# Query weights fused from DMA-transposed raw blocks, and the first two tiles of each layer without the residual sum on TensorE

## The chip, the cores and the metric

The kernel runs on one NeuronCore of a Trainium2 chip. The core has a matrix engine (TensorE, PE in the profile; its weight loads are the row PEld), a vector engine (VectorE, DVE), an activation engine (ScalarE, ACT), a general engine (GpSimd, POOL) and a queue engine (SyncE, SP) from which all DMA of this kernel is issued. The engines run their instruction streams in order and meet at semaphores. The metric is the device time of one execution in microseconds, as the median of several runs.

## What is computed

Two layers, each a linear attention (A) with softmax feature maps and a bilinear gated block (B). Both layers use the same weights. There are 2048 rows (16 tiles of 128), a width of 576, 32 heads of 18, and a hidden width of 4608.

```python
def A(x, wqkv, w_phi, wo):
    q, k, v = split_heads(x @ wqkv)                       # each (32 heads, 2048, 18)
    pq = einsum("bhsd,hdf->bhsf", q, w_phi)               # the kernel folds w_phi into wq and wk
    pk = einsum("bhsd,hdf->bhsf", k, w_phi)
    phi_q = concat([softmax(pq), softmax(-pq)])
    phi_k = concat([softmax(pk), softmax(-pk)])
    kv = einsum("bhsf,bhsd->bhfd", phi_k, v)
    z  = einsum("bhsf->bhf", phi_k)
    o = einsum("bhqf,bhfd->bhqd", phi_q, kv) / (einsum("bhqf,bhf->bhq", phi_q, z)[..., None] + 1e-6)
    return merge_heads(o) @ wo

def B(x, w_gate, w_up, w_down):
    return ((x @ w_gate) * (x @ w_up)) @ w_down

for _ in range(2):
    x = x + A(layernorm(x), ...)
    x = x + B(layernorm(x), ...)
```

Since q = LN(x) wq and pq = q w_phi per head, pq = LN(x) Wq with Wq = wq times a block-diagonal matrix of w_phi. That product, made once at the start for the q and for the k columns of wqkv, is called the fusion below.

## The kernel before

A Python scheduler records all instructions. Each piece of the work is a generator ("thread") that yields operations with rough durations, waits for events and takes buffers from pools; the scheduler places whichever can begin first by its own estimate. What it places is fixed in the program: on the chip each engine runs its list in that order. So a change of one thread also changes where the others stand.

The stages: all 16 tiles pass the k side of layer 1 (normalise, project to k and v, two softmaxes, add to kv); then a barrier masks kv into the block-diagonal BD; then for each pair of tiles the q side gives the attention output, and a block of gate and up projections (a "row") follows, then the down product. While a row runs, projections of other tiles are put between its matmuls. The k side of layer 2 runs inside the rows of layer 1.

The fusion for q and k, one 128-row block (kt) of the raw weights at a time. The rows of BDphi are in five groups of seven heads (126 columns):

```python
def t_fuse(self, which):
    ...
    if which == "q":
        yield ("wait", ("ain", 1, s.fq))                  # fq = 1: after tile 1 of the k side
    yield ("go", s.t_fuse2(which), ...)
    for kt in range(5):
        wt = yield ("acq", "wt")                          # two buffers
        (_, bank), = yield ("acqn", ["pb"], 1)
        # PE: 5 transposes of Wraw[:, kt, 126 columns] into one bank
        # ACT: 2 copies, bank -> WT[:, wt]
        yield ("rel", "pb", bank)

def t_fuse2(self, which):
    for kt in range(5):
        for half in range(2):
            (_, bank), = yield ("acqn", ["pb"], 1)
            # PE: groups 0..2 or 3..4: bank[:, c:c+n] = WT[:, wt, t, :]^T @ BDphi[:, t, 0:n]
            # ACT or DVE: copy of 378 or 198 columns, bank -> Wq[:, kt]
```

The load thread brings raw q weights with five loads after the sixth pair of x tiles; all transfers stand in one SP queue:

```python
for b in range(3, NB):
    yield ("wait", ("xT", 1, b - 3))
    yield from xload(b)
    if b == 5:
        for kt in range(5):
            yield from rawload("q", kt)
    if b == 6:
        yield from w5(s.Wo, s.A_wo, "Wo", "wo")
```

A query projection of a later tile, made ahead and stored, takes one of NPQ = 2 tokens and two of the eight PSUM banks:

```python
def t_qproj(self, L, st_):
    ...
    tok = yield ("acq", "pq")
    gots = yield ("acqn", ["pb"], 2, True)
    yield from s.proj(st_, s.Wq, "Wq", banks)             # 10 matmuls of 288 columns
    # ACT: 2 copies, bank -> xT[st_] (reused as store)
    yield ("rel", "pq", tok)
```

Tiles 0 and 1 of a layer lie on the way to the first row. Their attention output is transposed on TensorE, and before the change their residual sum is made there:

```python
def t_aout(self, L, st_):
    ...                                                   # numerator and denominator in 2 banks
    alts = [("dve", den)]                                 # +1e-6, reciprocal
    if st_ < 2: alts.append(("act", lnd))                 # or Ln and Exp on ScalarE
    # DVE: 2 products o = num * (1/den)
    if st_ < 2:
        # PE: 6 transposes of o, ACT: copy to oT
        for h in range(2):
            # PE: bank[h] = ident^T @ x_sb[st_, half h]   (start=True, stop=False)
        for h in range(2):
            yield from s.proj(..., s.Wo, ..., h, False)   # added to the same bank
        yield ("sig", ("xp", L, st_))
        for h in (1, 0):
            # ACT: copy bank[h] -> x_sb
        yield ("wait", ("bn", ...)); release both banks
        return
    # other tiles: proj, then DVE: x_sb = bank + x_sb
```

The normalisation of these two tiles (t_ln with fast=True) takes its statistics from the PSUM banks as soon as "xp" is signalled:

```python
src = s.ps[:, banks[h], 0:288] if banks else x_sb[...]
Op(bn_stats(st, src))                                     # DVE, 2 of them
...                                                       # aggregate, Ln, Exp, x -> xln (576 columns)
# PE: 6 transposes of xln, ACT: copy to xT
```

Of the kernel before, what the change touches and what calls it, by code (L numbers as in the profile page):

```python
# [491 lines left out]
NP = NF // 2  # L492
# [56 lines left out]
class K:  # L549
    def __init__(self, nc, A_x, A_wqkv, A_w_phi, A_wo, B_w_gate, B_w_up, B_w_down, out):  # L550
# [16 lines left out]
        self.NPQ = 2  # L567
# [3 lines left out]
        self.fq = 1  # L571
# [13 lines left out]
    def alloc(self):  # L585
# [5 lines left out]
        self.eps6 = A("eps6", [128, 1], F32)  # L591
        self.mask9 = A("mask9", [128, NK, GH], BF16)
        self.BD = A("BD", [128, NK, GH, CW], BF16)
        self.kvacc = A("kvacc", [128, NK, KW], F32)
        self.x_sb = A("x_sb", [128, NS, D], BF16)
# [16 lines left out]
        self.mask = AT("mask", [TW, TW], BF16, a0 + 1280 + 512 + 192)  # L612
        self.wdr = A("wdr", [128, self.NWD, CH, D], BF16)
# [43 lines left out]
        sc.pool("pq", self.NPQ)  # L657
# [7 lines left out]
        self.xbank = {}  # L665
# [6 lines left out]
        self.g_out = g("out")  # L672
        self.g_et = [g("et%d" % i) for i in range(self.NET)]
        self.g_ot = [g("ot%d" % i) for i in range(self.NOT)]
        self.raw_keys = [("mask",), ("BDphi",), ("onesf",), ("wst",), ("WT", 0), ("WT", 1)] + [("Wraw", 0, w_, k_) for w_ in ("q", "k") for k_ in range(5)]
# [12 lines left out]
    def t_init(self):  # L688
# [3 lines left out]
            Op(100, lambda e: e.memset(s.eps6[:], 1e-6), writes=[("eps6",)]),  # L692
            Op(200, lambda e: e.memset(s.Wk[:, 4, :], 0.0), writes=[("Wk", 0)]),
        ])
# [49 lines left out]
    def t_load(self):  # L744
# [24 lines left out]
        yield from grp("wphi", items, ("ld", "wphi"))  # L769
        for kt in range(5):  # L770
            yield from rawload("k", kt)
# [10 lines left out]
        for b in range(3, NB):  # L782
            yield ("wait", ("xT", 1, b - 3))
            yield from xload(b)
            if b == 5:
                for kt in range(5):
                    yield from rawload("q", kt)
            if b == 6:
                yield from w5(s.Wo, s.A_wo, "Wo", "wo")
# [14 lines left out]
    def t_fuse(self, which):  # L804
# [4 lines left out]
        if which == "q":  # L809
            yield ("wait", ("ain", 1, s.fq))  # L810
        yield ("go", s.t_fuse2(which), s.fqp if which == "q" else 8, "fuse2" + which)
        for kt in range(5):
# [16 lines left out]
            yield ("sig", ("wt", which, kt))  # L829

# [33 lines left out]
    blocks5 = [(k, 0, 128, 128 * k + 128) for k in range(4)] + [(4, 0, 64, 576), (4, 64, 128, 576)]  # L864

    def t_ln(self, tiles, sig, fast=False, slot=None, banks=None):
# [14 lines left out]
        for j in js:  # L883
            for h in range(2):
                if banks is None:
                    src, rd, ex = x_sb[:, ss[j], 288 * h:288 * h + 288], [("x", ss[j], 0), ("x", ss[j], 1)], []
                else:
                    src, rd, ex = s.ps[:, banks[h], 0:288], [("pbd", banks[h])], [("pb", banks[h])]
                ops.append(Op(d_dve(288), (lambda e, j=j, h=h, src=src: e.bn_stats(st[:, sl[j], 6 * h:6 * h + 6], src)),  # L889
                              reads=rd, writes=[("st", sl[j], h)], excl=ex))  # L890
        yield ("ops", "dve", ops)
        if banks is not None:
            yield ("sig", ("bn",) + sig[0])
# [15 lines left out]
        for j in js:  # L909
# [8 lines left out]
                                                                 ALU.add, ALU.mult)) for a, b, c in ((0, 576, 0), (576, 640, 512))[:2 - fast]]  # L918
            yield ("alt", [(eng, [Op(d, em[i], reads=[("x", ss[j], 0), ("x", ss[j], 1), ("nmean", sl[j]), ("rstd", sl[j])], writes=[("xln", sl[j])]) for i, d in enumerate(dur)])
                           for eng, dur in (("pool", (800, 200)[:2 - fast]), ("dve", (400,)))[:1 + fast]] + ([("act", act)] if boot else []))  # L920
        for j in js:
            if fast:
                (_, bank), = yield ("acqn", ["pb"], 1)
                P = s.psb16[bank]
                yield ("ops", "pe", [Op(60, (lambda e, j=j, k=k, P=P, r0=r0, r1=r1, c1=c1: e.transpose(P[r0:r1, 128 * k:128 * k + 128], xln[:, sl[j], 128 * k:c1], s.ident[:])),
                                        reads=[("xln", sl[j]), ("ident",)], writes=[("pbd", bank)], excl=[("pb", bank)]) for k, r0, r1, c1 in s.blocks5])
# [13 lines left out]
    def proj(self, st_, Wm, km, banks, src=None, keys=None, only=None, fresh=True):  # L940
# [4 lines left out]
        full = [Op(d_pe(N), (lambda e, k=k, h=h: e.matmul(s.ps[:, banks[h], 0:N], L[:, k, :], Wm[:, k, N * h:N * h + N], start=(k == 0 and fresh), stop=(k == 4))),  # L945
# [78 lines left out]
    def t_qproj(self, L, st_):  # L1024
# [6 lines left out]
        tok = yield ("acq", "pq")  # L1031
# [8 lines left out]
        yield ("rel", "pq", tok)  # L1040
# [110 lines left out]
    def t_kv(self, b):  # L1151
# [4 lines left out]
        for bi in range(3):  # L1156
# [10 lines left out]
            else:  # L1167
                em = (lambda e, pv=pv, kv=kv: e.tensor_tensor(kv, pv, kv, ALU.add))
            yield ("ops", "dve", [Op(d_dve(3 * KW), em, reads=[("kv", bank)] + ([("kvacc", bi)] if b else []),
                                     writes=[("kvacc", bi)], excl=[("pb", bank)])])  # L1170
# [6 lines left out]
    def t_barrier(self, L):  # L1177
# [3 lines left out]
        for bi in range(3):  # L1181
# [9 lines left out]
            yield ("alt", [(eng, [Op(dur, em, reads=rd + [("mask9",)], writes=[("BD", bi)], excl=ex)])  # L1191
# [6 lines left out]
    def t_aout(self, L, st_):  # L1198
# [40 lines left out]
        for i, (k, j, h, n) in enumerate(todo):  # L1239
# [10 lines left out]
        nv = [s.ps[:, bank, 0:16 * CW].rearrange("p (h c) -> p h c", c=CW) for bank in banks]  # L1250
        denk = [("den", ob, 0), ("den", ob, 1)]
        den = [Op(d_dve(16) + 80, (lambda e, i=i: e.tensor_scalar(s.den[:, ob, 16 * i:16 * i + 16], nv[i][:, :, DH:CW].rearrange("p h c -> p (h c)"), 1e-6, None, ALU.add)),
                  reads=[("pbd", banks[i])], writes=[("den", ob, i)], excl=[("pb", banks[i])]) for i in range(2)]
        den.append(Op(6.3 * 32 + 10, (lambda e: e.reciprocal(s.den[:, ob, :], s.den[:, ob, :])), reads=denk, writes=denk))
        alts = [("dve", den)]
        if st_ < 2:
            lnd = [Op(210, (lambda e, i=i: e.activation(s.den[:, ob, 16 * i:16 * i + 16], nv[i][:, :, DH:CW].rearrange("p h c -> p (h c)"), ACTF.Ln, bias=s.eps6[:, 0:1])),
                      reads=[("pbd", banks[i]), ("eps6",)], writes=[("den", ob, i)], excl=[("pb", banks[i])]) for i in range(2)]
            lnd.append(Op(230, (lambda e: e.activation(s.den[:, ob, :], s.den[:, ob, :], ACTF.Exp, scale=-1.0)), reads=denk, writes=denk))
            alts.append(("act", lnd))  # L1260
        yield ("alt", alts)
# [6 lines left out]
        if st_ >= 2:  # L1268
            ops.append(Op(130, (lambda e: e.tensor_copy(o[:, 576:640], o[:, 512:576])), reads=okeys, writes=okeys))
# [5 lines left out]
        if st_ < 2:  # L1275
            (_, bank), = yield ("acqn", ["pb"], 1)
            P = s.psb16[bank]
            yield ("ops", "pe", [Op(60, (lambda e, k=k, P=P, r0=r0, r1=r1, c1=c1: e.transpose(P[r0:r1, 128 * k:128 * k + 128], o[:, 128 * k:c1], s.ident[:])),
                                    reads=okeys + [("ident",)], writes=[("pbd", bank)], excl=[("pb", bank)]) for k, r0, r1, c1 in s.blocks5])
# [15 lines left out]
        if st_ < 2:  # L1295
            s.xbank[(L, st_)] = banks
            for h in range(2):
                bank = banks[h]
                yield ("ops", "pe", [Op(d_pe(288), (lambda e, h=h, bank=bank: e.matmul(s.ps[:, bank, 0:288], s.ident[:], s.x_sb[:, st_, 288 * h:288 * h + 288], start=True, stop=False)),
                                        reads=[("ident",), ("x", st_, 0), ("x", st_, 1)], writes=[("pbd", bank)], excl=[("pb", bank)])])  # L1300
            for h in range(2):
                yield from s.proj(st_, s.Wo, "Wo", banks, s.oT[:, oTb, :, :], [("oT", oTb)], h, False)
# [9 lines left out]
            for bank in banks:  # L1312
                yield ("rel", "pb", bank)
# [379 lines left out]
```

## Time and profile before

| | us |
|---|---|
| median of 3 runs | 1116.06 (1114.43 to 1116.64) |
| span of the profiled execution | 1114.3 |
| PE / DVE / ACT / POOL busy in it | 1072.3 / 592.0 / 376.5 / 311.5 |
| first gate matmul of layer 1 | 119.11 |
| last down matmul of layer 1 to first gate matmul of layer 2 | about 620.4 to 654.74 |

How to read the profile: times are microseconds from the start of the span. The page gives busy time of each engine, then the span in 40 slices of 27.9 us with one digit each (9 is 90% or more). In a line of the timeline stand the start, the busy time, the engine, the line of the kernel (L856), the operation, output and inputs, their shapes, the count, and in brackets the idle time of the engine just before and what ended it. In a table by stretch a line holds the stretch and its length, then busy time and instruction count for PE, PEld, DVE, ACT and POOL, the clock granted to TensorE, the DMA share and GB/s. In the chain of waits a line holds a start, a duration, an engine and a group. Names: ss are softmax sums, mxmn maxima and minima, dd the exponentials, psb the projections in SBUF, st the layernorm statistics, xln the normalised rows, xT and oT transposed rows.

### The profile page before, as it was taken

The numbers are of one execution on the slowest core, as the hardware profiler recorded it, in microseconds if no ns is written. First come the engines' busy times: TensorE is split into PE (matmuls) and PEld (weight loads), VectorE is DVE, ScalarE is ACT, GpSimd is POOL, SyncE is SP. The second block draws the span as 40 slices with busy tenths as digits, with TensorE's granted clock in tenths as the row PEclk, the third lists the DMA queues.
The fourth block names the chain that finished last, engine by engine and source line by source line (L and its number), as shares of the span: only waits on it lengthen the run. The fifth ranks groups of instructions, "written<-read, shape, count | busy, mean of one in ns | idle before, by whom it ended". The sixth has DMA issues, their size and how long they took to land.

```text
span 1114.3 us, 33775 instructions
## 1 busy us (share of the span) xinstructions
PE 1072.3 (96%) x15300; PEld 837.1 (75%) x15362; DVE 592.0 (53%) x1190; ACT 376.5 (34%) x867; POOL 311.5 (28%) x332
## 2 busy tenths in 40 slices
PE   5798999999999999999999899999999999999998
PEld 4566886868687786868787678696969696969685
DVE  7798744647466564646443575444535353524231
ACT  7786631414233241414332463131313130402120
POOL 5595512414242332413321252121212030300000
PEclk9699999999999999999999999999999999999999
DMA  8952127273452637262532313817272726262504
GB/s 191 265 210 65 28 43 204 47 202 49 138 107 73 156 37 199 47 191 39 138 89 78 115 24 47 214 36 215 36 209 41 192 58 192 58 177 52 181 24 139
DMA packets 181034, 128.23 MB, mean 115 GB/s; under 512 B 99354, under 2 KB 179738, under 8 KB 179738
## 3 DMA queue, kind: packets, MB, share of 16 engines
q1 hardware_dynamic: 180890, 126.07, 44.3%
q8 instruction: 120, 1.97, 0.7%
q14 instruction: 24, 0.20, 0.1%
HBM read 100.73 MB, written 2.36 MB: 93 GB/s over the span
## 4 chain that ended last, share of the span: by engine, by line
PE 82%; DVE 9%; ACT 4%; DMA 2%; issue 1%; POOL 1%; SPq 0%; DVEq 0%; ACTq 0%
PE ps L1383 46%; PE ps L1453 20%; PE ps L957 6%; PE ps L1456 4%; PE ps L945 3%; DVE ss L1072 2%; PE ps L1244 1%; DVE dd L1004 1%; PE ps L1125 1%; ACT hT L1429 1%; DMA oT<-dd 1%; DVE hT L1431 1%; DMA wdr<-in_B_w_down_dram 1%; DVE mxmn L990 1%; DVE mxmn L985 1%
## 5 line engine op out<-in xcount | busy, mean ns | idle before, releaser
L1383 PE MATMUL ps<-xT,Wu 64*128 64x256 bf16 x4608 | 581.9, 269 | 0.0
L1383 PE MATMUL ps<-xT,Wg 64*128 64x256 bf16 x4608 | 580.2, 269 | 0.8 <-ACT xT L927 0.8
L1383 PEld LDWEIGHTS ps<-xT,Wu 64*128 64x128 bf16 x4608 | 431.7, 94 | 22.6 <-DVE hT L1431 1.6
L1383 PEld LDWEIGHTS ps<-xT,Wg 64*128 64x128 bf16 x4608 | 427.5, 94 | 27.0 <-issue 3.3
L1429 ACT CAST hT<-ps 128x512 bf16<-128x512 f32 x288 | 167.9, 583 | 567.3 <-PE ps L1383 532.6
L1431 DVE TENSOR_TENSOR hT<-ps,hT 128x512 bf16<-128x512 f32 x288 | 196.9, 689 | 216.8 <-ACT hT L1429 216.0
L1453 PE MATMUL ps<-wdr,hT 128*128 128x512 bf16 x913 | 237.2, 380 | 0.4 <-DMA wdr<-in_B_w_down_dram 0.4
L1383 PE MATMUL ps<-xT,Wr 64*128 64x256 bf16 x1152 | 188.2, 269 | 0.0
L1456 PE MATMUL ps<-wdr,hT 128*128 128x64 bf16 x960 | 185.0, 193 | 2.8 <-issue 0.3
L1453 PEld LDWEIGHTS ps<-wdr,hT 128*128 128x128 bf16 x960 | 93.8, 98 | 109.6 <-DMA wdr<-in_B_w_down_dram 1.0
L1083 POOL TENSOR_TENSOR dd<-dd,ss 128x576 bf16<-128x576 bf16 x118 | 136.4, 1179 | 130.0 <-ACT ss L1079 123.0
L1054 POOL TENSOR_TENSOR dd<-xT,mxq 128x576 bf16<-128x576 bf16 x56 | 63.9, 1163 | 321.6 <-DVE mxq L1050 321.6
L1478 DVE TENSOR_TENSOR x_sb<-ps,x_sb 128x512 bf16<-128x512 f32 x32 | 22.0, 686 | 224.0 <-PE ps L1456 224.0
L917 POOL TENSOR_SCALAR xln<-x_sb,nmean,rstd 128x576 bf16<-128x576 bf16 x104 | 62.6, 607 | 172.4 <-ACT rstd L906 108.4
L1072 DVE TENSOR_REDUCE ss<-dd 128x64 f32<-128x1152 bf16 x61 | 82.2, 1348 | 26.3 <-ACT dd L1066 26.0
L1456 PEld LDWEIGHTS ps<-wdr,hT 128*128 128x128 bf16 x960 | 94.3, 98 | 0.0
L1383 PEld LDWEIGHTS ps<-xT,Wr 64*128 64x128 bf16 x1152 | 81.3, 94 | 5.2
L1064 ACT ACTIVATE dd<-dd 128x576 bf16<-128x576 bf16 x61 | 41.7, 684 | 48.9 <-DVE dd L1004 31.8
L1453 PE MATMUL ps<-wdx,hT 128*128 128x512 bf16 x177 | 50.8, 380 | 0.0
L995 POOL TENSOR_TENSOR dd<-psb,mxmn 128x576 bf16<-128x576 bf16 x24 | 27.9, 1164 | 77.0 <-DVE mxmn L985 77.0
L889 DVE BATCH_NORM_STATS2 st<-x_sb 128x6 f32<-128x288 bf16 x120 | 46.0, 445 | 3.7 <-DMA x_sb<-in_A_x_dram 3.6
L957 PE MATMUL ps<-Wo,oT 64*128 64x288 bf16 x504 | 43.5, 283 | 1.4 <-DMA oT<-dd 0.5
(118 smaller groups left out, 979.3 us busy)
## 6 DMA issues: line engine op xcount, KB each, us to landing
wdr<-in_B_w_down_dram SPq DMA_DIRECT2D x240, 288.0 KB, 3.5
wdx<-in_B_w_down_dram SPq DMA_DIRECT2D x48, 288.0 KB, 3.5
Wg<-in_B_w_gate_dram SPq DMA_DIRECT2D x4, 1152.0 KB, 15.3
Wu<-in_B_w_up_dram SPq DMA_DIRECT2D x4, 1152.0 KB, 17.6
x_sb<-in_A_x_dram SPq DMA_DIRECT2D x8, 288.0 KB, 3.2
out_dram<-x_sb SPq DMA_DIRECT2D x16, 144.0 KB, 2.3
Wraw<-in_A_wqkv_dram SPq DMA_DIRECT2D x8, 144.0 KB, 3.2
xT<-xln SPq DMA_TRANSPOSE x58, 2.7
```

What stands on the lines that cost most here:

```text
L889: ops.append(Op(d_dve(288), (lambda e, j=j, h=h, src=src: e.bn_stats(st[:, sl[j], 6 * h:6 * h + 6], src)), reads=rd, writes=[("st", sl[j], ...
L917: em = [(lambda e, j=j, a=a, b=b, c=c: e.tensor_scalar(xln[:, sl[j], a:b], x_sb[:, ss[j], c:c + b - a], s.nmean[:, sl[j]:sl[j] + 1], rstd[ ...
L957: out.append(Op(61, (lambda e, h=h, k=k, st=(i == 0 and k == 0), sp=(i == 1 and k == 3): e.matmul(s.ps[:, banks[h], 0:N], L[r, k, :], Wm[r ...
L1054: yield ("ops", "pool", [Op(1150, (lambda e, d=d, mb=mb: e.tensor_tensor(d, p3, mb, ALU.subtract)), reads=[("xT", st_), ("mq", mq, br)], w ...
L1064: yield ("ops", "act", [Op(590, (lambda e: e.activation(de2, de2, ACTF.Exp, scale=-1.0)), reads=s.ddk(sm, 1), writes=s.ddk(sm, 1))])
L1072: Op(1320, (lambda e: e.tensor_reduce(ss[:, sm, :].rearrange("p (b g) -> p b g", b=2), e4, AX.X, ALU.add)), reads=s.ddk(sm, 0) + s.ddk(sm, ...
L1083: yield ("alt", [(eng, [Op(dur, (lambda e, ev=ev, rb=rb: e.tensor_tensor(ev, ev, rb, ALU.mult)), reads=s.ddk(sm, br) + [("ss", sm)], write ...
L1383: out.append(Op(54.3, (lambda e, bank=bank, cs=cs, lhsT=lhsT, rhs=rhs, st=st, sp=sp: e.matmul(ps[:, bank, cs].rearrange("p (a n) -> p a n" ...
L1429: yield ("ops", "act", [Op(540, (lambda e, gb=gb, p=p: e.copy(hT[:, p, :], ps[:, gb, :])), reads=[("gu", gb)], writes=[("hT", p)] + (s.raw ...
L1431: yield ("ops", "dve", [Op(625, (lambda e, ub=ub, p=p: e.tensor_tensor(hT[:, p, :], ps[:, ub, :], hT[:, p, :], ALU.mult)), reads=[("gu", u ...
L1453: ops.append(Op(d_pe(512), (lambda e, lhsT=lhsT, bank=bank, slot=slot, fi=fi, f=f: e.matmul(ps[:, bank, 0:512], lhsT, s.wslot(slot)[:, fi, ...
L1456: ops.append(Op(d_pe(64) + 3, (lambda e, lhsT=lhsT, sl=sl, slot=slot, fi=fi, f=f: e.matmul(ps[:, Z, 64 * sl:64 * sl + 64], lhsT, s.wslot(s ...
```

## The change

Raw q weights are no longer transposed on TensorE. For each of the five row blocks a DMA transpose writes five blocks of 128 columns to WTq, a new tile that lies over BD and kvacc, which are not yet in use then. The block-diagonal matrix for q is built a second time in the layout of these blocks (BDphi5, one GpSimd product; eight heads touch each block of 128 columns). Products of one half (288 columns) go to one bank and one copy to Wq. The wait fq + fqs * kt lets block kt go after tile 3, 5, 7, 9 or 11 of the k side, so that the fusion is spread over it. It is meant to take transposes and copies off TensorE and ScalarE and to stop the fusion from coming as one piece. The k weights keep the old way.

```diff
-        self.NPQ = 2
-        self.fq = 1
+        self.fq = 3
+        self.fqs = 2
+        self.WTq = AT("WTq", [128, 5, 5, 128], BF16, nc.lookup_mloc(self.BD).addr)
+        self.wst5 = AT("wst5", [128, 5, DH], BF16, ...)
+        self.BDphi5 = AT("BDphi5", [128, 5, GH, DH], BF16, ...)
...
             if b == 5:
+                yield from grp("wphi5", late, ("ld", "wphi5"))
                 for kt in range(5):
                     yield from rawload("q", kt)
+                    yield ("dma", s.g_wq[kt], (... dma_start_transpose(s.WTq[:, kt, :, :], s.Wraw[:, kt, 0:640])),
+                           [("Wraw", 0, "q", kt), ("Wraw", 0, "k", kt)], [("WTq", kt)], ...)
...
+    def t_fuseq(self):
+        yield ("wait", ("ld", "wphi5"))
+        yield ("ops", "pool", [... BDphi5 = wst5 * mask9 ...])
+        for kt in range(5):
+            yield ("wait", ("ld", "raw", "q", kt))
+            yield ("wait", ("ain", 1, s.fq + s.fqs * kt))
+            for half in range(2):
+                (_, bank), = yield ("acqn", ["pb"], 1)
+                # PE: for each block k with heads of this half:
+                #     bank[:, c:c1] = WTq[:, kt, k, :]^T @ BDphi5[:, k, a:b, :]
+                # ACT or DVE: one copy of 288 columns to Wq[:, kt]
```

The second part takes back the residual sum on TensorE for tiles 0 and 1, the statistics from PSUM, the choice of ScalarE for the denominator and the six-piece transposes (five of 128 columns again, so that the last 64 columns are copied to columns 576 to 640 first). The sum is made by VectorE as for all other tiles, and the normalisation may go to GpSimd or VectorE.

```diff
-        tok = yield ("acq", "pq")
         gots = yield ("acqn", ["pb"], 2, True)
...
-        if st_ < 2:                                   # in t_aout
-            (PE: bank = ident^T @ x_sb, then proj adds; ACT copies to x_sb; banks held for bn_stats)
-            return
         yield from s.proj(st_, s.Wo, "Wo", banks, s.oT[:, oTb, :, :], [("oT", oTb)])
         (DVE: x_sb = bank + x_sb, two halves)
...
-                    src = s.ps[:, banks[h], 0:288]    # in t_ln
+                    x_sb[:, ss[j], 288 * h:288 * h + 288]
...
-            yield ("alt", alts)                       # den on DVE or on ACT
+            (DVE: +1e-6, reciprocal)
-        if st_ >= 2:
-            ops.append(copy o[:, 512:576] -> o[:, 576:640])
+        ops.append(copy o[:, 512:576] -> o[:, 576:640])
...
-                yield ("wait", ("xp", L, 0))          # start of tile 0's normalisation
+            yield ("wait", ("x1", L, 2 * b))
```

## The prediction

> **What bounds the kernel now.** I read the page's utilisation rows first, then busy time by stretch, then the timeline where a stretch is not bound by TensorE, then the chain of waits.
>
> ```profile
> PE 1072.3 (96%) x15300; PEld 837.1 (75%) x15362; DVE 592.0 (53%) x1190; ACT 376.5 (34%) x867; POOL 311.5 (28%) x332
> ...
> PE   5798999999999999999999899999999999999998
> ...
> DVE  7798744647466564646443575444535353524231
> ```
>
> From the fifth slice TensorE is full. The change cannot shorten that body except by moving work out of it. Only slices 1 to 4 (the k side of layer 1) and the change of layers near 620 us leave TensorE room. The first gate matmul starts at 119.11 us, and 995 us follow it. By stretch the start looks so (engine columns in the order PE, PEld, DVE, ACT, POOL):
>
> ```profile
> 36.00:48.60 12.60, 7.58 (x57) 5.33 (x56) 7.71 (x20) 7.82 (x21) 5.04 (x6) 0.57 0.93 205
> 48.60:60.00 11.40, 10.51 (x88) 7.98 (x86) 10.83 (x20) 8.85 (x25) 8.39 (x8) 0.87 0.99 412
> 60.00:72.00 12.00, 11.69 (x104) 8.23 (x102) 12.00 (x22) 10.49 (x29) 11.85 (x11) 1.00 0.81 336
> 72.00:84.00 12.00, 10.03 (x97) 7.35 (x95) 12.00 (x22) 8.60 (x23) 12.00 (x12) 1.00 0.01 3
> ```
>
> From 60 to 84 us VectorE and GpSimd are both full: one tile takes 3.4 us (the sums L1072 follow each other at 57.49, 60.89, 64.36 ...). From 36 to 48.6 us nothing is full. There the query weights are fused:
>
> ```profile
> 39.97 0.88 ACT L824 COPY WT<-ps 126x512 bf16<-126x512 bf16 x2 [1.76 <-PE ps L821]
> 40.28 0.55 DVE L856 CAST Wq<-ps 128x378 bf16<-128x378 f32 x1 [0.63 <-PE ps L843]
> 41.29 0.36 DVE L856 CAST Wq<-ps 128x198 bf16<-128x198 f32 x1 [0.45 <-PE ps L843]
> 42.24 0.55 DVE L856 CAST Wq<-ps 128x378 bf16<-128x378 f32 x1 [0.59 <-PE ps L843]
> 43.23 0.36 DVE L856 CAST Wq<-ps 128x198 bf16<-128x198 f32 x1 [0.44 <-PE ps L843]
> 44.80 0.55 DVE L856 CAST Wq<-ps 128x378 bf16<-128x378 f32 x1 [1.20 <-PE ps L843]
> ...
> 48.59 1.33 DVE L1072 TENSOR_REDUCE ss<-dd 128x64 f32<-128x1152 bf16 x1
> ```
>
> TensorE, ScalarE and VectorE hand each other one block at a time, and between the softmax sums of 38.31 and 48.59 us VectorE does nothing but Wq copies and waits. The other part of the change is in the tail, from the mask product of kv at 105.08 to 119.11 us, 14.0 us, a chain over tiles 0 and 1:
>
> ```profile
> 109.77 0.95 DVE L1266 TENSOR_TENSOR dd<-ps,den 128x288 bf16<-128x288 f32 x2
> 111.30 0.46 DVE L889 BATCH_NORM_STATS2 st<-ps 128x6 f32<-128x288 f32 x1
> 112.22 0.47 DVE L889 BATCH_NORM_STATS2 st<-ps 128x6 f32<-128x288 f32 x1 [0.47 <-ACT x_sb L1308]
> 113.67 0.43 DVE L917 TENSOR_SCALAR xln<-x_sb,nmean,rstd 128x576 bf16<-128x576 bf16 x1 [0.56 <-ACT rstd L906]
> 117.91 0.69 ACT L927 COPY xT<-ps 128x640 bf16<-128x640 bf16 x1 [0.82 <-PE ps L925]
> ```
>
> Statistics are read from PSUM 0.9 us apart, because ScalarE copies the same bank between them: the sum on TensorE is not free. In the chain of waits, a query projection inside a gate row shows as two pieces:
>
> ```profile
> 123.21 0.61 PE ps L957 x10
> 123.83 1.09 PE ps L1383 x20
> 124.92 0.49 PE ps L957 x8
> ```
>
> So it costs the full row 0.61 + 0.49 = 1.1 us (1.3 later in that row).
>
> [...] five blocks on TensorE take 0.74 to 0.80 us plus 0.88 us of ScalarE copies, and a 128x640 DMA transpose holds the SP queue about 1.3 us and lands after 2.7. [...] So a transpose that waits for its raw weights holds back what stands behind it; the queue's own waits here (102 us in all for GpSimd's xln) fit that. [...]
>
> **Part 1, the fusion.** Out go 25 transposes, 25 products and 10 WT copies. In come 30 products of 36 to 144 columns, 10 Wq copies of 288 columns, five DMA transposes and one GpSimd product of 720 elements, an estimate of 1.16 x 720/576 = 1.45 us. In the changed order 3 Wq copies stand on VectorE and 7 on ScalarE. VectorE saves 4 x (0.55 + 0.36) - 2 x 0.40 = 2.8 us, and 0.75 us more since one max subtraction moves to GpSimd. The softmax chain no longer stops at 39 us. Walking VectorE's new order with the durations above from the sum at 25 us gives the sums of tiles 1 to 5 at 29, 33, 38, 41 and 44.5 us: tile 5 is done at 45.8, where it was done at 58.8 before. But two statistics of x (tiles 12 to 15, 2.0 us each with aggregate) have been put off behind it, and they wait for loads that stand on SP behind the last WTq transpose. SP: 21 us, then three rounds of raw load, xT pair, WTq (0.5 + 2.6 + 1.3), then two rounds that wait for the landing (3.2) give about 46 us; x lands at 49.5 to 50. VectorE waits some 4 us there, and the sum of tile 7 ends near 60.9 instead of 65.6. After that both run 3.4 us a tile. Two late Wq copies cost 0.75 us and the moved subtraction gives that back. So the mask product comes near 100.4 instead of 105.1: **-4.7 us**.
>
> **Part 2, the tail of layer 1.** In the new order tile 1's transposes and numerator stand behind tile 0's numerator and output projection, so the two tiles are less overlapped: the second numerator starts 6 to 7 us after the mask product, not 3.2. Tile 0 then needs two residual additions on VectorE (0.45 each) before two statistics, and a copy of 64 columns (0.18); its normalisation falls to GpSimd, 1.3 against 0.43 us. Adding along the path: oT of tile 1 at +11, its projection to +13.3, additions and statistics to +15, normalised at +16.3, transposed at +16.9, then two projections in TensorE's order: gate matmuls at about +19.3, against +14.0. **+5.3 us**. The start is then 100.4 + 19.3 = 119.7, nearly where it was.
>
> **Part 3, work moved out of rows.** Without the two-token limit 14 query projections of layer 1 instead of 11 stand ahead of the first row, so that 2 are inside it, not 5: 3 x 1.2 = **-3.6 us**. In layer 2 two fewer: **-2.3 us**.
>
> **Part 4, the change of layers.** The same freedom puts two projections (2.4 us) between tile 14's transposes and its k projection, which before waited 0.81 us for ScalarE, so it slips 1.6 us; the same before tile 15, together 2.6 to 3.2. The tail of tiles 0 and 1 loses 0.9 us by the additions. **+3.5 us**.
>
> Sum: -4.7 + 5.3 - 3.6 - 2.3 + 3.5 = -1.8; 1116.1 - 1.8 is about **1114 us**.
>
> **Rivals.** (a) The late x loads take the whole place of the pause: if x lands at 53 us, part 1 is worth about 1 us and the kernel takes 1118. The strict SP order speaks for it, the 45.8 us at which VectorE gets there against it. (b) The tail costs less: if TensorE's last projections find the gate work ready late anyway, part 2 is +2 and the time 1110. VectorE's idle time in the old tail (3.3 of 14.1 us) speaks for it. (c) GpSimd becomes the bound of the start: it gets 1.45 + 1.16 us more and is full from 60 to 84 us; with nothing regained while VectorE waits, 1116.5. Its 7.6 idle microseconds from 36 to 48.6 speak against. (d) A late start of the gate weight loads: 28 us of loading from about 60 us is done by 95, ahead of 119. I give it little.
>
> **Range and chances.** Each of parts 1, 2 and 4 may be off by 2 to 3 us, together some 4.5; so 1108 to 1120. Two per cent is 22 us, five times that spread: nearly all chance is on the same.
>
> **What would show it.** Right: no stretch of paired Wq copies; the sum of tile 5 near 45 us with a VectorE wait on the x load right after; the mask product at 99 to 102; first gate matmul at 118 to 121; layer 2's about 3.5 us later after the last down product than the 34.3 of before; 2 and 0 query projections inside the first rows. Wrong: a first gate matmul before 116 or after 123, or a wait of TensorE on WTq or on gate weights.

## The result, and the profile after

The changed kernel takes 1121.98 us (1121.17 to 1124.06), 1.0058 times the time before, 95% interval 1.0040 to 1.0075. That is 5.8 us more, outside the predicted range. A second set of runs gave 1.0062 (1.0048 to 1.0076). The first lines of the page after:

```profile
PE 1072.3 (96%) x15222; PEld 832.0 (74%) x15284; DVE 592.9 (53%) x1198; ACT 370.7 (33%) x854; POOL 316.0 (28%) x337
...
PE   6687999999999999999999889999999999999998
...
DVE  7888744647375664546352567353535353534231
...
PEclk9999999999999999999999989999999999999999
```

TensorE is busy for 1072.3 us, to a tenth of a microsecond as long as before, although it has 78 matmuls fewer; some of those that are left ran at a lower granted clock (0.50, 0.59 and 0.62 in stretches shown below), and what was added to the span is time in which it stands. The slices show where. Slices 2 to 4 (28 to 112 us) read 6, 8 and 7 instead of 7, 9 and 8. Slices 23 and 24, around the change of layers (617 to 673 us), read 8 and 8 instead of 8 and 9, and slice 24 has the only lowered clock of its row. All stages, taken from the timelines of two traces of the changed kernel (before / after, with the second trace in brackets):

| | before | after | difference | predicted |
|---|---|---|---|---|
| mask product of kv starts | 105.08 | 102.64 (104.14) | -2.4 (-0.9) | -4.7 |
| from there to the first gate matmul ("the tail") | 14.0 | 19.4 (19.4) | +5.3 (+5.3) | +5.3 |
| first row of layer 1 | 46.4 | 42.8 (42.6) | -3.6 (-3.8) | -3.6 |
| first down product to last down product of layer 1 | 455.1 | 455.9 (455.3) | +0.8 (+0.2) | 0 |
| last down product to layer 2's first gate matmul ("the change of layers") | 34.2 | 40.9 (39.2) | +6.7 (+5.0) | +3.5 |
| first row of layer 2 | 42.7 | 43.0 (42.8) | +0.3 (+0.1) | -2.3 |
| the rest | 416.9 | 417.7 (417.7) | +0.8 (+0.8) | 0 |

The differences add up to 7.9 us in the first trace and 6.6 in the second, as single executions do; the medians are 5.8 us apart.

The fusion went much as described up to 50 us. VectorE's timeline of the changed kernel:

```profile
46.25 1.35 DVE L1102 TENSOR_REDUCE ss<-dd 128x64 f32<-128x1152 bf16 x1 [0.29 <-ACT dd L1096]
...
50.97 1.54 DVE L921 BATCH_NORM_STATS2 st<-x_sb 128x6 f32<-128x288 bf16 x4 [1.00 <-DMA x_sb<-in_A_x_dram]
...
59.35 1.35 DVE L1102 TENSOR_REDUCE ss<-dd 128x64 f32<-128x1152 bf16 x1 [0.70 <-ACT dd L1096]
...
61.99 0.75 DVE L1015 TENSOR_REDUCE mxmn<-psb 128x32 f32<-128x576 bf16 x1 [0.56 <-ACT psb L1012]
...
64.35 1.35 DVE L1102 TENSOR_REDUCE ss<-dd 128x64 f32<-128x1152 bf16 x1 [0.88 <-ACT dd L1096]
...
81.82 0.45 DVE L864 CAST Wq<-ps 64x288 bf16<-64x288 f32 x1 [1.14 <-PE ps L858]
```

There are no more pairs of Wq copies. The sum of tile 5 starts at 46.25 (57.49 before; 44.5 was predicted), the wait for x is 1.0 us instead of four, and tile 7's sum ends at 60.70 (60.9 was predicted). That the two agree is partly luck: the sums came 1.0 to 1.8 us later than worked out, and the shorter wait made up for it. Then come waits where full load was expected. The sum after it starts 5.0 us later (59.35 to 64.35) instead of 3.4, and at 81.82 VectorE waits 1.14 us for a product of the fusion. The first of these has to do with TensorE's timeline just before:

```profile
57.27 0.72 PE L858 MATMUL ps<-BDphi,WTq 128*128 128x144 bf16 x6 [5.19 <-DVE dd L1034]
57.80 1.40 PE L975 MATMUL ps<-Wv,xT 128*128 128x288 bf16 x5
58.99 2.53 PE L975 MATMUL ps<-Wk,xT 128*128 128x288 bf16 x10
...
63.18 1.39 PE L975 MATMUL ps<-Wk,xT 128*128 128x288 bf16 x10
```

TensorE stood 5.2 us with a product of the new fusion at the head of its queue, which waits for VectorE to leave a PSUM bank. When it came back, a k projection took 2.53 us that takes 1.39 at 63.18; the granted clock was 0.50 from 56 to 61 us and 1.00 from 62 to 65. In the change of layers the timeline of TensorE holds tile 15's k projection and then the products into kv, before:

```profile
628.57 1.40 PE L945 MATMUL ps<-Wk,xT 128*128 128x288 bf16 x10 [0.81 <-ACT xT L927]
...
639.13 1.18 PE L1125 MATMUL ps<-vx,dd 128*128 128x152 bf16 x17 [1.61 <-POOL dd L1083]
640.14 2.62 PE L945 MATMUL ps<-Wq,xT 128*128 128x288 bf16 x20
```

and after:

```profile
630.27 2.62 PE L975 MATMUL ps<-Wq,xT 128*128 128x288 bf16 x20 [0.51 <-DVE dd L1034]
632.73 1.39 PE L975 MATMUL ps<-Wk,xT 128*128 128x288 bf16 x10
...
641.93 0.37 PE L1155 MATMUL ps<-vx,dd 128*128 128x152 bf16 x3 [0.68 <-POOL dd L1113]
643.03 0.58 PE L1155 MATMUL ps<-vx,dd 128*128 128x152 bf16 x8 [0.73 <-DVE kvacc L1198]
644.34 0.57 PE L1155 MATMUL ps<-vx,dd 128*128 128x152 bf16 x6 [0.73 <-DVE kvacc L1198]
644.75 4.29 PE L975 MATMUL ps<-Wq,xT 128*128 128x288 bf16 x20
```

Two query projections (x20) stand ahead of the k projection, as predicted, and ahead of tile 14's likewise (1.7 us later after the last down product than before). Not predicted: kv comes in four pieces, two of which wait until VectorE has emptied a bank, and after it 20 matmuls take 4.29 us instead of 2.62, at a granted clock of 0.59 (in the second trace 2.61, at 1.00). Then the first row of layer 2 starts at a low clock as well (0.62). By stretch, its first 4.5 us after (columns as before: busy time and count of PE, PEld, DVE, ACT, POOL, clock, DMA share, GB/s):

```profile
661.50:666.00 4.50, 4.47 (x52) 3.43 (x54) 1.31 (x2) 0.69 (x3) 3.70 (x4) 0.62 0.04 8
```

### The profile page after: what moved, and what is told of

Read it like the earlier page. It is cut to its first block, busy times and chain, and to the rows that moved or that the text cites. A ratio compares the mean times of both kernels' runs of the same rounds, so it can differ in the third digit from the quotient of the medians.

```text
span 1122.3 us, 33634 instructions
## 1 busy us (share of the span) xinstructions
PE 1072.3 (96%) x15222; PEld 832.0 (74%) x15284; DVE 592.9 (53%) x1198; ACT 370.7 (33%) x854; POOL 316.0 (28%) x337
## 4 chain that ended last, share of the span: by engine, by line
PE 80%; DVE 9%; DMA 4%; ACT 4%; POOL 1%; issue 1%; SPq 1%; DVEq 0%; POOLq 0%; ACTq 0%
PE ps L1386 45%; PE ps L1456 20%; PE ps L987 5%; PE ps L1459 4%; PE ps L975 2%; DMA oT<-dd 2%; PE ps L1274 1%; DVE ss L1102 1%; PE ps L1155 1%; DVE hT L1434 1%; POOL dd L1113 1%; ACT hT L1432 1%; DMA wdr<-in_B_w_down_dram 1%; DVE x_sb L1322 1%; DVE dd L1034 1%
## 5 line engine op out<-in xcount | busy, mean ns | idle before, releaser
L1025 POOL TENSOR_TENSOR dd<-psb,mxmn 128x576 bf16<-128x576 bf16 x26 | 30.2, 1163 | 78.2 <-DVE mxmn L1015 78.2
L921 DVE BATCH_NORM_STATS2 st<-x_sb 128x6 f32<-128x288 bf16 x128 | 49.3, 446 | 4.4 <-DMA x_sb<-in_A_x_dram 4.2
```

The lines of the kernel that those rows point to most:

```text
L921: ops.append(Op(d_dve(288), (lambda e, j=j, h=h: e.bn_stats(st[:, sl[j], 6 * h:6 * h + 6], x_sb[:, ss[j], 288 * h:288 * h + 288])), reads= ...
```

## The experiments

The theory when they began: the missing tokens cost in the change of layers, the PE sum taken back costs in the tail, and the fusion gains a little. The change has three parts that can be set one by one: F, the new fusion; T, the tokens gone; P, the PE sum taken back with all that goes with it. All eight combinations have run, and nine further kernels or repetitions. The table holds all of them; the columns after the ratio come from one timeline of each, in us.

| kernel | time | ratio to before (95%) | mask product | tail | row 1 | change of layers | row 1 of layer 2 |
|---|---|---|---|---|---|---|---|
| before | 1116.1 | 1 | 105.1 | 14.0 | 46.4 | 34.2 | 42.7 |
| F (f_only) | 1114.99 | 0.9984 (0.9977 to 0.9991) | 102.4 | 14.5 | 46.4 | 34.2 | 42.5 |
| P (p_only) | 1116.44 | 0.9997 (0.9989 to 1.0005) | 105.8 | 14.2 | 46.2 | 35.0 | 41.7 |
| T (t_only) | 1123.00 | 1.0061 (1.0045 to 1.0078) | 104.5 | 18.6 | 42.8 | 38.9 | 41.9 |
| F, P (f_p) | 1117.64 | 1.0009 (1.0002 to 1.0016) | 104.2 | 15.1 | 46.1 | 35.0 | 41.7 |
| F, T (f_t) | 1120.07 | 1.0028 (1.0018 to 1.0037) | 102.3 | 18.8 | 42.6 | 40.4 | 41.6 |
| T, P (t_p) | 1120.76 | 1.0043 (1.0029 to 1.0058) | 104.3 | 15.8 | 44.5 | 39.2 | 41.1 |
| F, T, P (after_2) | 1123.97 | 1.0062 (1.0048 to 1.0076) | 104.1 | 19.4 | 42.6 | 39.2 | 42.8 |
| T in layer 1 only (t_l1) | 1118.37 | 1.0016 (1.0009 to 1.0024) | 104.6 | 18.6 | 42.8 | 34.2 | 42.5 |
| three tokens (n3) | 1127.67 | 1.0093 (1.0079 to 1.0107) | 105.2 | 17.2 | 47.3 | 40.3 | 42.9 |
| T, k side first (t_kfirst) | 1127.70 | 1.0101 (1.0087 to 1.0115) | 106.1 | 18.6 | 42.8 | 41.5 | 43.3 |
| F, one token (f_n1) | 1122.72 | 1.0066 (1.0051 to 1.0081) | 105.4 | 14.2 | 47.3 | 35.0 | 47.3 |
| F, x loads first (f_x) | 1119.84 | 1.0030 (1.0018 to 1.0041) | 106.6 | 14.5 | 46.4 | 34.2 | 42.5 |
| F, T, P, filled (after_fill) | 1123.39 | 1.0067 (1.0053 to 1.0080) | 102.2 | 19.4 | 42.8 | 40.7 | 41.4 |
| the same again (after_fill_2) | 1123.37 | 1.0051 (1.0035 to 1.0066) | 103.8 | 19.4 | 42.6 | 39.2 | 41.1 |
| F again (f_2), one run | 1114.34 | | 102.9 | 14.5 | 46.1 | 34.2 | 42.3 |
| F, P again (f_p_2), one run | 1119.00 | | 105.5 | 15.1 | 45.9 | 35.0 | 41.5 |

### The parts alone

```diff
 F:  -fq = 1   +fq = 3, fqs = 2, WTq, BDphi5, t_fuseq, five DMA transposes
 T:  -tok = yield ("acq", "pq")   -yield ("rel", "pq", tok)
 P:  -the branch "if st_ < 2" of t_aout, bn_stats from PSUM, six-piece transposes
```

> The kernel before with the new fusion of the query weights alone (DMA transposes, BDphi5, blocks after tiles 3 to 11); the residual sum on TensorE and the two tokens stay. Theory (the fusion gains a little at the start and is not the loss): mask product near 102.6 us as in the changed kernel, first gate matmul 14.0 us later at 116.6, the rest as before: -2.4 us, about 1113.7. Rival 'the fusion itself is the loss' (late x loads, WTq over BD and kvacc): first gate matmul at 119 or later, 1116 to 1119. Part 1 as predicted: mask product 100.4, time 1111.4.

F gains: 0.9984, 1.8 us, with the mask product at 102.43. It is not the loss.

> The kernel before with the two tokens for stored query projections taken away alone. Theory (this is what costs at the change of layers): first gate matmul of layer 1 at 119.1 as before; first row of layer 1 shorter by 3.6 us (2 projections in it instead of 5); from the last down matmul of layer 1 to the first gate matmul of layer 2 about 40 us instead of 34.3; clock below 0.9 in some stretch there; first row of layer 2 no shorter than before although it has two projections fewer. Sum -3.6 + 5.7 + 0.3 = +2.4, about 1118.5. Rival 'the tokens are free and the PE sum is the loss': change of layers 37, first row of layer 2 shorter by 2.3; -3.6 + 2.7 - 2.3 = -3.2, about 1113.

T alone costs 6.2 us by the medians (1123.00 against 1116.85 in that set; the ratio gives 6.8), more than the theory's 2.4 and as much as the whole change. The change of layers grew by 4.7 us (5.7 was expected), but the tail grew too, by 4.6 us, with the PE sum still in place. That half was not in the theory.

> The kernel before with the residual sum on TensorE (with its statistics from PSUM, the choice for the denominator and the six-piece transposes) taken back alone; the old fusion and the tokens stay. Theory: mask product at 105.1 as before, first gate matmul 19.4 us after it at 124.5 (+5.4); change of layers about 35.2 (+0.9), where one projection more stands ahead of the row (-1.2 in the row, +1.2 ahead of it): +6, about 1122. Rival 'the tail has slack': first gate matmul at 121 to 122, +2 to +3, about 1119. Rival 'the PE sum is nearly the whole loss and the tokens cost nothing': +8 to +9, 1125, since the fusion gives back 2.4.

P alone costs nothing (0.9997), so the theory and both its rivals fall. Its tail is 14.2 us. This is its TensorE timeline from the mask product (105.81) on:

```profile
107.23 1.40 PE L1232 MATMUL ps<-BD,eT 128*128 128x152 bf16 x24
...
111.11 1.40 PE L933 MATMUL ps<-Wo,oT 128*128 128x288 bf16 x10 [0.78 <-ACT oT L1262]
```

Both numerators stand together at 107.23 (24 matmuls). In the kernel with the tokens gone alone, which keeps the PE sum, tile 1's stands behind tile 0's output projection:

```profile
105.94 0.79 PE L1242 MATMUL ps<-BD,eT 128*128 128x152 bf16 x12
...
109.89 1.39 PE L943 MATMUL ps<-Wo,oT 128*128 128x288 bf16 x10
111.11 0.78 PE L1242 MATMUL ps<-BD,eT 128*128 128x152 bf16 x12
```

That divides all runs: where tile 1's numerator precedes tile 0's output projection the tail is 14.0 to 15.8 us (before, F, P, both, T with P, one token, x first); where it follows, 17.2 to 19.4 (T, F with T, the changed kernel with and without filling, T in layer 1, three tokens, k side first).

> The changed kernel with the two tokens given back: fusion and PE sum as changed. Theory: mask product near 102.6, first gate matmul near 122; first row of layer 1 back to 46.4; change of layers about 35.2 with a clock of 0.95 or more throughout, first row of layer 2 about 41.5 to 42.7. -2.4 + 6 = +3.6, about 1119.7, that is 2.3 us faster than the changed kernel although it has three projections more in layer 1's first row. Rival 'the tokens are free, the rest is the loss': without their gain the kernel gets slower than the changed one, 1124 to 1126. Rival 'the clock drop comes by chance or from the fusion': clock below 0.9 again in the first microseconds of layer 2's first row.

The changed kernel with its tokens back: 1.0009, 4.9 thousandths below the first result of the changed kernel (1.0058), 5.5 us. The change of layers is 35.0, and 35.0 in its second trace too, where the granted clock is 1.00 throughout. More than the theory's 2.3, and against the rival.

> The changed kernel with the residual sum on TensorE left as it was before: fusion new, tokens gone. Theory (without tokens the tail is long with or without the PE sum): mask product 102.4, first gate matmul 18.6 us later near 121.0, first row 42.8, change of layers 39 to 40.5, first row of layer 2 42 to 43: 1119.5 to 1121. Rival, part 2 as predicted (the PE sum taken back makes the tail 5.3 us longer): first gate matmul at 117, 1116. In that case the PE sum is the main loss after all.

The theory holds against part 2's reading: with the PE sum in place the first gate matmul is at 121.10, 18.8 us after the mask product. In the same set it is 3.9 us faster than the changed kernel.

### What the tokens held

```diff
 t_l1:  -tok = yield ("acq", "pq")   +tok = (yield ("acq", "pq")) if L == 2 else None
 n3:    -self.NPQ = 2                +self.NPQ = 3
 f_n1 (on F):  -self.NPQ = 2         +self.NPQ = 1
```

> The kernel before, with the two tokens taken away in layer 1 only; layer 2 keeps them. Theory (the projections moved out of the first row of layer 1 only move into the tail ahead of it and hold tile 1 back there): first gate matmul near 123.1 as with the tokens gone in both layers (before: 119.1), first row 42.8 instead of 46.4, first down product +0.5; a microsecond lost in layer 1's body again; change of layers 34.2 and first row of layer 2 42.7 as before: +0.5 to +1.5, 1117.3 to 1118.3. Rival, part 3 as predicted (three projections out of the row are 3.6 us gained): 1113.

As expected: the row is 3.5 us shorter and the tail 4.6 longer; 1.6 us lost. Between the first numerator and the first gate matmul stand seven query projections instead of four: three more of 1.23 us are 3.7 of the 4.6 us.

> The kernel before with three tokens instead of two. The program has the same five projections inside layer 1's first row, so nothing is moved out of it; but tile 1's numerator stands behind tile 0's output projection, as in all kernels without tokens. Theory (a third stored projection in flight takes banks from tile 1): mask product to first gate matmul 16.5 to 18.5 us instead of 14.0, row 46.4 as before, change of layers 36 to 40: 1121 to 1126. Rival (the tail grows only by the projections moved ahead of the row): tail 14.0, change +1.2 to +2.4 by the order, 1118 to 1119.

This separates the two readings of that tail. With three tokens four projections stand there, as before, and the tail still grows to 17.2 us, because tile 1 comes late. The three extra ones of T fill the gap that this leaves and add the rest. The programs show why tile 1 is late, in the numbers of the PSUM banks that their matmuls write. With two tokens tile 1's numerator writes bank 4, which held tile 6's projection, and bank 0, which held tile 0's numerator. With three tokens the projection of tile 8 has banks 1 and 2, which the mask product has left, that of tile 9 has banks 7 and 4, both from tile 6's projection, and tile 1 writes banks 3 and 5: it waits until tile 7's projection is copied out. Without tokens (T) the banks are the same as with three. In layer 2 tile 1 also falls behind with three tokens (first numerator to gate matmul 17.2 us, 12.2 before). The time, 1127.67, is above both expectations, since the change of layers (40.3) and the first row (47.3) grew too; why they did stays open.

> The new fusion alone with one token instead of two, PE sum kept: three stored projections fewer stand ahead of the first gate matmul of each layer. Theory (few of them in flight let tile 1 follow tile 0 at once, the projections left out are paid for later in the rows): mask product to first gate matmul 12.5 to 14 us, change of layers 32.5 to 34, but 2 to 4 us more in rows and downs of each layer: 1114 to 1117, no better than two tokens (0.9984 of before). Rival (fewer is better): 1112.

One token is too few: the tails stay short (14.2), but the projections come back into the rows: 47.3 and 47.3 us, and 4.4 us more between layer 1's first and last down product. Both expectations were too good. Two is the best of one, two, three and none that ran; one ran with F only, three and none without it.

> The kernel before without the two tokens, but in layer 2 a query projection waits until the k projection of tile 15 has been placed. It puts the k side first and leaves the number of PSUM banks that projections may hold free. Theory A (the order in front of tiles 14 and 15 costs it): tile 14's k projection 3 to 4 us after the last down product instead of 5.7, kv in at most two pieces, change of layers near 34.5, no stretch below 0.9 clock, first row of layer 2 42.7: about 4 us better than without tokens (1123.0), so 1119. Theory B (held banks cost it): kv still in three or four pieces that wait for VectorE's kvacc, change of layers 36.5 to 38, 1121 to 1122.

```diff
 in t_qproj, tokens gone:   +if L == 2: yield ("wait", ("kp", 2, NS - 1))
```

Neither theory, and 1127.70 is slower than both said: kv was finished 22.0 us after the last down product (24.1 without tokens, 19.7 before), so the order is part of it. But TensorE then had nothing to do ahead of tile 14, waited 2.77 us, after which ten matmuls took 2.58 us instead of 1.39, and in the tail of layer 2 the projections that had been held back now pushed tile 1 behind tile 0 (17.3 us against 12.4). What is held back at one place stands in the way at the next.

### The clock

```diff
 in the changed kernel, layer 2, tiles 0 and 1:
 +yield from s.t_fill(banks[0], 6)      # ahead of the output projection
 +yield from s.t_fill(bank, 8)          # ahead of the transposes of xln
 +# t_fill: n matmuls of 288 columns into a bank that is overwritten next
```

> The changed kernel with 28 matmuls of 288 columns added whose result is overwritten: in layer 2, tiles 0 and 1, six ahead of each output projection and eight ahead of each transposition of the normalised rows, where TensorE waits for ScalarE or VectorE (0.6 to 1.1 us each time). They do no useful work. Theory (TensorE's idling lowers its clock into the first row of layer 2): the clock in the first 5 us of that row is 0.9 or more instead of 0.62, first row 40.5 to 41 us instead of 43.0; change of layers 40.9 to 41.4; the kernel gets 2 us faster although TensorE has 3.4 us more to do, about 1120. Rival (the lower clock has another cause, or costs nothing): first row 43 again, change of layers +0.3, 1122 to 1122.6.

> The changed kernel once more, to stand beside the next one under the same conditions. 1121.5 to 1123; clock near 0.62 in the first 5 us of layer 2's first row and that row 43.0 us, as in its first trace, if the lower clock belongs to the kernel and not to chance.

> The changed kernel with the 28 idle-time matmuls in layer 2's tail, once more beside the changed kernel itself. Theory: first row of layer 2 41.4 against 43.0, change of layers within 0.3, so 1.0 to 1.8 us faster than the changed kernel in the same set of runs. Rival (the shorter row in one trace was chance, or is given back later): within 0.5 us of it.

By stretch, the first 4.5 us of layer 2's first row, of the changed kernel in its second trace and of the filled one in its first:

```profile
660.55:665.05 4.50, 4.50 (x54) 3.32 (x56) 1.27 (x2) 0.65 (x3) 3.74 (x4) 0.63 0.05 10
```

```profile
661.40:665.90 4.50, 4.50 (x84) 4.02 (x86) 1.87 (x3) 1.42 (x4) 3.88 (x4) 1.00 0.10 19
```

84 matmuls instead of 54 in the same time (84 in the second trace too), and a row shorter by 1.7 and 1.6 us in the two traces, with useless work added and the change of layers no longer. So TensorE's idling ahead of the row has a part in its low clock. The spans of the traces fall by 1.1 us each. The times don't show it: the first set, at 1123.39, is not the 1120 that was expected, and in the set that has both kernels they differ by 0.6 us, far within their intervals. So the clock costs 1.6 us in the row where the traces show it, and whether that reaches the time is not shown. Nor does idling alone decide it: T with P has the same order of TensorE's work and the same waits in that tail, kept 1.00, and ran its row in 41.1.

### The start of the fused kernels

```diff
 f_x (on F):  loads of x for tiles 12 to 15 and of Wo ahead of
              -the five raw loads and transposes to WTq
```

> The kernel before with the new fusion alone, and in it the last two loads of x ahead of the five raw loads and DMA transposes of the q weights (they stood behind them). Theory (in the fusion alone VectorE has no wait for x left; what it loses after 58 us is TensorE standing for a PSUM bank and coming back at half clock): mask product at 101.5 to 103, within 1 us of 1115.0. Part 1's own picture (late x loads stop VectorE): mask product near 100.4, about 1113. Against: the fused blocks come later, and if their copies collide with the full stretch, 1116.

With the x loads early, the mask product comes 4.2 us later (106.6), and no expectation had that. The new place of the loads gave the scheduler another order: VectorE now waits 2.29 us for ScalarE in each of three pairs of tiles:

```profile
70.14 1.35 DVE L1116 TENSOR_REDUCE ssx<-ddx 128x64 f32<-128x1152 bf16 x1 [2.29 <-ACT ddx L1110]
79.28 1.35 DVE L1116 TENSOR_REDUCE ss<-dd 128x64 f32<-128x1152 bf16 x1 [2.29 <-ACT dd L1110]
```

So this run does not measure what the late loads cost. The traces do: VectorE's wait for x is at most 1.0 us (changed kernel), and 0.21 us or less in the two of F.

> The changed kernel with the old fusion: tokens gone, PE sum taken back. It completes the eight combinations of the three parts. A (the PE sum matters where tile 1 lags for want of tokens, that is in the tails): mask product near 105, first gate matmul 20 us later or more, change of layers 41: 3 us above the kernel without tokens (1.0061 of before), near 1.009. B (its extra cost with the new fusion comes from the start of the fused kernels, which has two forms, mask product near 102.4 or near 104.1): within 1 us of the kernel without tokens, near 1.006 to 1.007.

1.0043 is below both readings and nearer to B. So no cost of P shows in kernels with the old fusion, with or without tokens. With tokens gone the ratio is even lower with P, and tile 1 keeps its place in the trace, but the intervals overlap. With the new fusion P costs 2.7 us (F to F, P) and 3.9 us (F, T to the changed kernel).

> The new fusion alone, one more look at its start. Until the mask product its engines have the same instructions in the same order as the fusion with the PE sum taken back (but for one memset of VectorE ahead of all). Theory (two forms of one start, decided by TensorE's clock after it waits at 53.6 to 57.7 us): mask product near 102.4 or near 104.1, and at 104.1 the k projection near 59.5 takes 2.6 us instead of 1.9. Rival (the form belongs to the program): 102.4 again.

> The fusion with the PE sum taken back and two tokens, one more look at its start: near 102.4 or near 104.1 by the same theory; near 104.1 again by the rival.

F and F with P have the same instructions in the same order on every engine up to the mask product, but for one memset. Their starts differ all the same, among other things by TensorE's clock between 60 and 64 us. By stretch, F in its first trace and F with P in its second:

```profile
60.00:64.00 4.00, 4.00 (x38) 3.23 (x37) 3.27 (x6) 2.73 (x8) 2.83 (x3) 0.95 1.02 226
```

```profile
60.00:64.00 4.00, 4.00 (x21) 2.68 (x19) 2.54 (x4) 2.40 (x6) 2.88 (x3) 0.50 0.92 206
```

38 matmuls in 4 us in the one, 21 in the other. Over the four traces, clocks of 0.95, 0.71 (F), 0.52 and 0.50 (F with P) go with mask products at 102.4, 102.9, 104.2 and 105.5: a range, not the two forms that were expected. The clock makes only a part of it. The fused product that waits for a bank starts at 57.7, 56.9, 57.9 and 59.5 us in these traces, so up to 2.7 us were there before it. From it to the mask product they take 44.7, 46.1, 46.3 and 46.0 us; the k projection behind it takes 1.87 us in the first and 2.61 in the others. In the changed kernel, with mask products at 102.6 and 104.1, 1.2 of the 1.5 us are there when that product starts (57.3 and 58.5).

So the start is not fixed by the program alone, and P does not decide it. Over ten traces of kernels with F (x loads first left out) the mask product comes at 102.3 to 105.4 without P and at 102.2 to 105.5 with P. Why P costs 2.7 us and more where the fusion is new stays open.

## Why the prediction was wrong, by its own steps

**Part 1, the fusion, -4.7: right in kind, half in size.** F alone gives -2.7 and -2.2 us at the mask product and 1.8 us in the time. The end of tile 7 came as said, though two of the steps to it were off and cancelled. The step that failed is "After that both run 3.4 us a tile". It took VectorE and GpSimd to be the only limit there and did not see that a product of the fusion, put between the projections, would stop TensorE for 4 to 5 us on a PSUM bank (5.19 us; 4.13 and 4.14 in F), nor that TensorE could come back from that at a granted clock of 0.50: the next sum came 5.0 us after tile 7's (4.3 in F, where the clock from 60 to 64 us was 0.95 against 0.84). A later product of the fusion then held VectorE for 1.14 us (1.13 and 1.14 in F). Rival (a), late x loads, gave a wait of 1.0 us and no more.

**Part 2, the tail, +5.3: right in size, and the size was partly luck.** The second numerator starts 6.8 us after the mask product, as the text read from the new order, and its walk along the path holds to within 1 us: tile 1's rows are normalised at +16.5 us (+16.3 was said), with two projections behind their transposes. But the text did not ask which part of the change makes that order, and it laid the rest of the length to the additions, the copy and the slower normalisation of P. P alone leaves the tail at 14.2; T alone, with the sum in place, makes it 18.6. What P adds to the tail is 0.2 us alone and 0.6 us with F, with or without tokens. Rival (b) rightly saw slack in the old tail, but its +2 and 1110 us did not come.

**Part 3, projections out of rows, -3.6 and -2.3.** The first row of layer 1 is shorter by 3.6, as said, but "ahead of the first row" is the tail, and 3.7 us of projections reappear there. They were counted as removed and only moved. In layer 2 two fewer give 1.6 us, not 2.3, where the clock stays at 1.00 (42.7 to 41.1 in T with P), and nothing in the changed kernel, where it is 0.62 in the row's first 4.5 us.

**Part 4, the change of layers, +3.5.** It was 6.7 (5.0 in the second trace). Tile 14 slips 1.7 us, as said. The same before tile 15 was put at 1.0 to 1.6 us more and is 2.4: two projections take 2.5 us, and the old wait of 0.81 us that they were to fill was replaced by waits of 0.18 and 0.51 us, by the trace for ScalarE and VectorE to empty a bank. The tail of tiles 0 and 1 adds 0.5 us, where 0.9 was said. The terms not seen are kv in pieces (0.5 us from tile 15's k projection to the end of kv) and, in the first trace only, two projections at a granted clock of 0.59 (1.7 us).

**The sum.** The tokens were worked out as a gain: -3.6 - 2.3 and most of +3.5, together about -3. By the ratios they cost 6.1 thousandths set alone (6.8 us), 4.4 with the fusion (4.9 us), 4.6 with the PE sum taken back (5.1 us), 5.3 with both (5.9 us, from the second set). That is the error, in every surrounding. The step that failed is to count a projection out of a row as time gained. In layer 1 three of them came back in the tail (3.7 us), and the freed order put tile 1 behind tile 0. In layer 2 two more stand ahead of the row (14 instead of 12, 2.5 of the 5.0 us), and the row gave back 1.6 us at most. A token was read as a limit on work; it also limits how many of the eight banks that work holds. For tile 1 in layer 1 the bank numbers show that; for kv in layer 2 it is argued, and worth 0.5 us by the trace. Of the signs that the prediction named, two and no projections inside the first rows came; the mask product (102.64) and the first gate matmul (122.01) lay outside what it called right, and in the second trace (123.50) the gate matmul lay in what it called wrong.

## What to carry to other kernels

A token, a depth or a pool size beside a queue of fill-in work is there for the resource that the work holds, not for the work: before it is taken away, ask who gets the next free PSUM bank at each barrier, and what the work will stand ahead of. A projection that leaves a full stretch has gained nothing until it is shown where it stands instead. And when a change has several parts, set each alone: here the part with the fewest lines made most of the loss, the largest one gained, and the version with the largest part alone, 0.9984 of the time before, is the best of all that ran.

## What the runs showed of the hardware that was not expected

TensorE's granted clock falls in a kernel in which it is busy 96% of the time. After waits of 5.19 us (to 57.27 us, granted clock 0.50 from 56 to 61 us) and 2.77 us (k side first) ten Wk matmuls took 2.53 and 2.58 us instead of 1.39. Ahead of layer 2's first row no single wait was longer than 1.14 us, and the clock fell to 0.62 behind a stretch with 3.08 busy us in 5.30:

```profile
654.70:660.00 5.30, 3.08 (x25) 2.07 (x25) 4.51 (x15) 2.95 (x8) 0.00 (x0) 1.00 0.02 3
```

The clock reads 1.00 in that stretch and 0.62 from 661.50 to 666.00 us, when TensorE is full again (4.47 busy us in 4.50). It need not come: T with P has the same 3.08 us with the same 25 matmuls ahead of its row (652.07 to 657.37 us) and kept 1.00, while T, with 3.64 us (654.06 to 659.36), fell to 0.62. The slow matmuls take nearly twice as long (2.61 against 1.39 us for ten), and how many are slow varies between executions: behind waits of 4.13 and 4.14 us the same ten matmuls of F took 1.87 us in one trace and 2.61 in the other. A single wait of that length was not needed in layer 2's tail. What else sets the clock, and after how much idling it falls, is not shown by these runs.
